# Attention scores as 64 by 64 quarters of the TensorE array instead of zero-padded full-array matmuls

## The chip, the core and the metric

The kernel runs on one NeuronCore of a Trainium2 chip. The metric is the time of one execution on the device in microseconds; lower is better. The engines named here are TensorE (PE for its matmuls, PEld for its weight loads), VectorE (DVE), ScalarE (ACT), GpSimd (POOL) and SyncE (SP), whose queue issues all the DMAs of this kernel.

## The reference

A local attention with block summaries is followed by two feed-forward blocks. Inputs are float32. There are 2 batches, 8 heads, 768 positions and a head size of 64.

```python
k_sum = k.reshape(B, H, nb, 32, D).max(axis=3)          # 24 blocks
v_sum = v.reshape(B, H, nb, 32, D).mean(axis=3)
scores_l = where(|i - j| < 16, q @ k.T / 8, -1e9)
scores_s = q @ k_sum.T / 8 + log(32)
a = softmax(concat([scores_l, scores_s]))
x = a @ concat([v, v_sum])                              # to (1536 tokens, 512)
x = x / sqrt(mean(x * x) + 1e-6) * rms_g
x = (silu(x @ w_gate) * (x @ w_val)) @ w_out            # d_ff 1536
h = x @ w_in
out = (s * relu(h) ** 2 + b) @ w_out2                   # d_ff 2048
```

## The kernel before, in words

**Attention.** The work is cut into 12 token tiles of 128 queries (index `i`; six to a batch) and 4 pairs of heads (`pr`), so 48 units. The two heads `e` of a pair lie on partitions 0 to 63 and 64 to 127 of queries and keys. A unit sees 192 key columns (`KC`): 24 block maxima, 8 columns of padding, 16 + 16 neighbours on both sides and the 128 keys of the tile itself. A unit passes these steps:

- `emit_a` (L317): two score matmuls in float32 (L328), one for each head. The stationary operand is a column block of `qz`, the queries of the tile. Each token tile's `qz` holds two zero-padded copies: in copy `e` only the 64 partitions of head `e` carry queries, and the others are zero, so that a matmul over all 128 partitions gives one head's scores. Both results go side by side into one PSUM bank. `top` (L333) then adds the mask on VectorE, writes the negated, scaled scores to the tile `P` in SBUF and leaves the maximum of each row in `sm`; `exps` (L339) takes the exponential on ScalarE with the row sums.
- `emit_b` (L345), three steps later: three transposes of `P` (L348), copied to `PT` by ScalarE or VectorE.
- `emit_c` (L361), six steps after the scores: three value matmuls (L367 to L369). After the fourth pair, `emit_d` normalises the token tile, and some ticks later `emit_e` (L396) transposes it for the feed-forward part.

**Order.** All is emitted in an order written by hand; every engine takes its instructions in that order. `attn` (L404) is a generator that yields twice a step: after `emit_b` and `emit_c`, and after `emit_a`. Each yield is a tick of the main loop (L640), which first runs what falls due (`run_due`). `after(d, fn)` puts `fn` in a list that is run d + 1 ticks on; `top` is put there with 1 and `exps` with 2. Between the ticks the main loop inserts groups of feed-forward matmuls (`gate` and `val`, twelve passes of 512 columns each), so that these begin while the attention goes on. Each group of them calls `run_due` too, through `slot` (L474).

**PSUM.** `banks(...)` hands out named banks in turn, and a bank taken again is waited for until all readers of its last contents are done. The scores take banks 0, 1 and 2 up to tick 20 (L631) and banks 0 and 1 after it (L644); the transposes use 3, 4 and 5 (later 3 and 4), the values 6 and 7, and the feed-forward groups 2 and 5.

**Queries.** There are two `qz` tiles, used in turn by the token tiles. `load_q` (L268) fills one with two DMAs of 64 partitions on the queue of SP; the load for tile `i + 2` is issued behind the scores of tile `i`. The zero halves are set once by four VectorE memsets at the start (L114, L115).

**Feed-forward.** From L615 on the rest of the two blocks runs, with float32 products as three float32r passes of hi and lo parts (L469 to L472, L601 to L604). It begins after the attention is done, and the change does not touch it.

Of the kernel before, what the change touches and what calls it, by code (L numbers as in the profile page):

```python
# [9 lines left out]
F32 = mybir.dt.float32  # L10
# [3 lines left out]
AF = mybir.ActivationFunctionType  # L14
ALU = mybir.AluOpType
AX = mybir.AxisListType
PSUM = bass.MemoryType.PSUM
# [3 lines left out]
NPAIR = NH // 2  # L21
NTL = SEQ // 128
# [3 lines left out]
KC = 192  # L26
# [10 lines left out]
def kernel(ctx: ExitStack, tc: tile.TileContext, q_t, k_t, v_t, v_w, w_gate, w_val, w_out, w_in2, w_out2, rms_g, s2, b2, out):  # L37
    nc = tc.nc
    scale = 1.0 / math.sqrt(HD)
# [16 lines left out]
    psp = pool("ps", 1, space=PSUM)  # L56

    def banks(*ids):
        """tiles of the PSUM banks ids, in turn"""
        turn = [0]  # L60

        def take():
            i = ids[turn[0] % len(ids)]
            turn[0] += 1
            return psp.tile([128, 512], F32, tag=f"b{i}", name=f"b{i}")
        return take
# [1 line left out]
    def r(ap):  # L68
        return ap.bitcast(F32R)

# [1 line left out]
    ident = const.tile([128, 128], F32, name="ident")  # L72
    mone = const.tile([128, NH], F32, name="mone")
    mhalf = const.tile([128, 1], F32, name="mhalf")
# [1 line left out]
    gbc = const.tile([128, DM], F32, name="gbc")  # L76
    sbc = const.tile([128, 1], F32, name="sbc")
    bbc = const.tile([128, 1], F32, name="bbc")
    qz = [const.tile([128, 2, NPAIR, 128], F32, name=f"qz{i}") for i in range(2)]
    part = const.tile([128, NSUB * 4 * SUB], F32, name="part")  # L80

    def big():
        return hgp.tile([128, NSUB * 2 * SUB], F32, tag="hg", name="hg")

    # keys and values of both batches lie where the products of the MoE come to lie later
    store = [big() for _ in range(5)] + [part[:, i * 3072:(i + 1) * 3072] for i in range(2)]
    kst = [t.rearrange("p (j c) -> p j c", c=KC) for t in (store[0], store[3], store[5])]
    vst = [t.rearrange("p (t a c) -> p t a c", t=3, a=NPAIR) for t in (store[1], store[2], store[4], store[6])]
# [2 lines left out]
    def kW(b, pr, t):  # L91
        j = (b * NPAIR + pr) * NTL + t
        return kst[j // 16][:, j % 16]

    def kpieces(b, pr):
        """runs of tiles of a pair's keys in one store: (store, slot, first tile, tiles)"""
        j = (b * NPAIR + pr) * NTL
        out, t = [], 0
        while t < NTL:
            n = min(NTL - t, 16 - (j + t) % 16)  # L100
            out.append((kst[(j + t) // 16], (j + t) % 16, t, n))
            t += n
        return out
# [6 lines left out]

    def consts():
        make_identity(nc, ident)
        for z in qz:
            nc.vector.memset(z[64:128, 0], 0.0)  # L114
            nc.vector.memset(z[0:64, 1], 0.0)  # L115
        for st in kst:
            nc.vector.memset(st[:, :, NS:BLK], 0.0)
        m = masks[1]
        nc.gpsimd.memset(m, 0.0)
        nc.gpsimd.memset(m[:, 0:NS], math.log(BLK) / scale)  # L120
        nc.gpsimd.memset(m[:, NS:BLK], NEG / scale)
        band(m, BLK, WIN, -WIN)
        band(m, BLK + WIN, WIN, 128)
        band(m, 64, 128, 0)
        for i, o in ((0, BLK), (2, BLK + WIN)):
            nc.vector.tensor_copy(masks[i], m)
            nc.vector.memset(masks[i][:, o:o + WIN], NEG / scale)
        nc.gpsimd.memset(mhalf, -0.5)
        nc.gpsimd.memset(mone, -1.0)
# [3 lines left out]
        nc.sync.dma_start(out=sbc, in_=s2.rearrange("(o d) -> o d", o=1).broadcast_to([128, 1]))  # L133
        nc.sync.dma_start(out=bbc, in_=b2.rearrange("(o d) -> o d", o=1).broadcast_to([128, 1]))

# [1 line left out]
    later = [[] for _ in range(8)]  # L137

    def after(d, fn):
        later[d].append(fn)  # L140
# [4 lines left out]
        for fn in due:  # L145
            fn()

# [1 line left out]
    order = []  # L149
    for m in range(KF):  # L150
        order.append(("s1", m))
# [26 lines left out]
        raw_t[i] = t  # L178

    def w_scale(i):  # L180
        """high words as float32 with their exponent moved: 2^-112 leaves five bits of it"""
        a = wap.tile([128, 512], F32, tag="wa", name="wa")
        nc.scalar.activation(out=a, in_=raw_t[i][:, :, 1].bitcast(F32), func=AF.Copy, scale=2.0 ** -112)
        a_t[i] = a

    def w_bits(i):
        """float32 of the float64 words: 23 bits of mantissa, the last one rounded to odd"""
        t = raw_t.pop(i)
        lo, hi = t[:, :, 0], t[:, :, 1]
        ai = a_t[i].bitcast(I32)  # L190
        ops = [
            lambda: nc.vector.tensor_scalar(out=ai, in0=ai, scalar1=3, scalar2=1, op0=ALU.logical_shift_left, op1=ALU.bitwise_or),
            lambda: nc.vector.scalar_tensor_tensor(out=ai, in0=hi, scalar=-0x80000000, in1=ai, op0=ALU.bitwise_and, op1=ALU.bitwise_or),  # L193
            lambda: nc.vector.scalar_tensor_tensor(out=ai, in0=lo, scalar=29, in1=ai, op0=ALU.logical_shift_right, op1=ALU.bitwise_or),  # L194
        ]
        pend[i] = ops

        def one():
            if ops:
                ops.pop(0)()  # L200
        one()
        if busy[0]:
            after(1, one)
            after(3, one)
        else:
            one()
            one()
# [27 lines left out]
                prog[j] += 1  # L235

    def w_ahead(part):
        """the weights' own work, between the work of the tokens"""
        i = used[0]
        if part == 0:  # L240
            w_to(i + 8, i + 7, 0, i + 5)
        elif part == 1:
            w_to(i + 8, 0, i + 6, 0)
# [6 lines left out]
        used[0] += 1  # L250
        return ready.pop(i)

# [1 line left out]
    vt_t = {}  # L254

    def load_k(b, pr):
# [9 lines left out]
        nc.sync.dma_start(out=vA[b][t].rearrange("p a c -> p (a c)"), in_=v_w[b, t])  # L266

    def load_q(i):  # L268
        z = qz[i % 2]
        for e in range(2):  # L270
            nc.sync.dma_start(out=z[64 * e:64 * e + 64, e].rearrange("p a c -> p (a c)"), in_=q_t[i, 64 * e:64 * e + 64])

    def prep_k(b, pr):
        ks = smallp.tile([128, NS], F32, tag="ks", name="ks")
# [10 lines left out]
        return vt_t[b][:, c0:c0 + 512].rearrange("p (a c) -> p a c", a=NPAIR)  # L285

    def prep_v(b, pr):
        """block means of the values, per column of the transposed values"""
        if pr == 0:
            nc.gpsimd.memset(vsums(b, 0), 0.0)  # L290
        vs = vsums(b, 1)[:, :, 0:NS]
        nc.vector.tensor_reduce(out=vs[:, pr], in_=vt_t[b][:, pr * SEQ:(pr + 1) * SEQ].rearrange("p (c i) -> p c i", i=BLK),
                                axis=AX.X, op=ALU.add)
        if pr == NPAIR - 1:
            for h in range(2):
                p0 = 64 * h
                nc.scalar.activation(out=vsums(b, 0)[p0:p0 + 64, :, p0:p0 + NS], in_=vs[p0:p0 + 64], func=AF.Copy, scale=1.0 / BLK)
# [16 lines left out]

    P_t, PT_t, X_t, xn_t, sm_t = {}, {}, {}, {}, {}

    def emit_a(i, pr, ps_s):  # L317
        t = i % NTL
        mk = masks[0 if t == 0 else 2 if t == NTL - 1 else 1]
        if pr == 0:  # L320
            sm_t[i] = smallp.tile([128, 2, NH], F32, tag="sm", name="sm")
        sm = sm_t[i]
        P = (tmpp.tile([128, 512], F32, tag="tmp", name="P") if i else wlp.tile([128, 512], F32, tag="wl", name="P"))
        P = P[:, 0:2 * KC].rearrange("p (e c) -> p e c", e=2)
        ps = ps_s()
        pv = [ps[:, e * KC:(e + 1) * KC] for e in range(2)]
        for e in range(2):
            nc.tensor.matmul(pv[e], qz[i % 2][:, e, pr], kW(i // NTL, pr, t), start=True, stop=True)  # L328

        def top():  # L330
            for e in range(2):
                h = 2 * pr + e
                nc.vector.tensor_tensor_reduce(out=P[:, e], in0=pv[e], in1=mk, op0=ALU.add, op1=ALU.min,  # L333
                                               scale=-scale, scalar=3.0e38, accum_out=sm[:, 0, h:h + 1])

        def exps():
            for e in range(2):
                h = 2 * pr + e
                nc.scalar.activation(out=P[:, e], in_=P[:, e], func=AF.Exp, scale=-1.0,  # L339
                                     bias=sm[:, 0, h:h + 1], accum_out=sm[:, 1, h:h + 1])  # L340
        after(1, top)
        after(2, exps)
        P_t[i, pr] = P

    def emit_b(i, pr, ps):  # L345
        P = P_t.pop((i, pr)).rearrange("p e c -> p (e c)")
# [55 lines left out]
        after(1, lambda: nc.vector.tensor_tensor(out=r(x[:, 1, :, c0:c0 + 128]), in0=pv, in1=x[:, 0, :, c0:c0 + 128], op=ALU.subtract))  # L402

    def attn(ps_s, ps_t, ps_x):  # L404
        """half a unit per step; yields the token tile that it completes"""
        loads = [lambda t=t: load_vw(0, t) for t in range(3, NTL)]
        loads += [lambda pr=pr: load_k(1, pr) for pr in range(NPAIR)]
        loads.append(lambda: load_vt(1))
# [31 lines left out]
        for s in range(n + LC):  # L440
# [14 lines left out]
                        emit_d(i)  # L455
            yield done
            if s < n:
                emit_a(*us[s], ps_s)
                i, pr = us[s]
                if pr == NPAIR - 1 and i + 2 < NT:  # L460
                    load_q(i + 2)
                yield

# [1 line left out]
    def mm12(ps, w, act):  # L465
        hi, lo = w
        for kk in range(4):
# [4 lines left out]
            nc.tensor.matmul(ps, r(hi[:, kk * 128:(kk + 1) * 128]), r(act(kk, 1)), start=False, stop=kk == 3)  # L472

    def slot(part):  # L474
        """what follows a group of products: the weights ahead, then older groups' work"""
        run_due()
        if phase:
            part = phase[0] = 1 - phase[0]
        if not busy[0]:
            w_ahead(part)  # L480
# [6 lines left out]
        return big().rearrange("p (s e c) -> p s e c", s=NSUB, e=2)  # L487

    def two(ps, dst, bias=None):
        """ps (+ bias) as a float32r pair"""  # L490
        if bias is None:
            nc.scalar.activation(out=r(dst[0]), in_=ps, func=AF.Copy)
            nc.vector.tensor_tensor(out=r(dst[1]), in0=ps, in1=dst[0], op=ALU.subtract)
# [2 lines left out]
            nc.vector.scalar_tensor_tensor(out=r(dst[1]), in0=ps, scalar=bias, in1=dst[0], op0=ALU.add, op1=ALU.subtract)  # L496

    def moe(x, ps_m):
        """x: a tile of (hi, lo) per part of the tokens"""
        hs, gs, y = {}, {}, []  # L500
        yp = part.rearrange("p (m s c) -> p m s c", m=KD, s=NSUB)
        op = part.rearrange("p (t c) -> p t c", t=NT)
# [112 lines left out]
        for kind, m in order:  # L615
            yield from {"s1": s1, "s2": s2, "s3": s3, "s4": s4}[kind](m)

# [1 line left out]
    consts()  # L619
    x = [xyp.tile([128, 2, KD, SUB], F32, tag="xy", name="x")]  # L620
    load_k(0, 0)
# [6 lines left out]
    for t in range(3):  # L628
        load_vw(0, t)
    load_small()  # L630
    m_banks, s_banks, t_banks = [banks(2, 5)], [banks(0, 1, 2)], [banks(3, 4, 5)]  # L631

    def ps_t():
        return t_banks[0]()
# [49 lines left out]
def _layout(q, k, v, moe_w_gate, moe_w_val, moe_w_out, moe_rms_g, moe2_w_in, moe2_w_out, moe2_s, moe2_b):  # L684
# [2 lines left out]
    c = np.ascontiguousarray  # L687

    def heads(a):
        # [b, h, s, d] -> [b, (e d), pair, s]  # L690
        return a.reshape(NB, NPAIR, 2, SEQ, HD).transpose(0, 2, 4, 1, 3).reshape(NB, 128, NPAIR, SEQ)

    qt = heads(q).reshape(NB, 128, NPAIR, NTL, 128).transpose(0, 3, 1, 2, 4)
# [63 lines left out]
```

## Time and profile before

| | |
|---|---|
| median of the runs shown (663.47 and 663.69) | 663.58 us |
| span of the profiled execution, first to last instruction | 662.4 us |
| the median over that span | 1.2 us more (the profiled execution's own time is not listed apart) |
| PE busy | 645.8 us, 97% of the span, 3140 passes |
| PEld busy | 547.7 us, 83% |
| DVE busy | 402.2 us, 61% |
| ACT busy | 272.6 us, 41% |
| POOL busy | 137.3 us, 21% |
| granted TensorE clock, mean | 0.997 of full |

Busy time counts the time in which an engine worked on at least one instruction. TensorE passes overlap (a pass is still on its way out while the next streams in), so a busy share near 100% says that the stream has no holes longer than such a tail, and the distance between two starts says what a pass costs. The profile lists one record for each pass; where the same kind of instruction follows itself, a timeline merges the records into one row with their count. A line number is that of the kernel above.

### The profile page before, as it was taken

To read this page: it belongs to the slowest core of one execution; us is meant where nothing else is said; L and a number is where in the kernel's file an instruction comes from. 1 tells how busy PE (TensorE), PEld (TensorE's weight loads), DVE (VectorE), ACT (ScalarE), POOL (GpSimd) and SP (SyncE) were. 2 spreads that over 40 slices of the span, in tenths; PEclk is the share of its full clock that TensorE was granted. 3 is DMA by queue.
4 is the path that set the end of the run, shared out by engine and by line. 5 is a ranking of instruction groups with operands and counts; after the bars stand their busy time and mean duration, and the time that the engine had idled before them with its cause. 6 is when DMAs were issued, how large, how long until landed. Compare 5 with 4: busy or idle time off the path is not lost.

```text
span 662.4 us, 8488 instructions
## 1 busy us (share of the span) xinstructions
PE 645.8 (97%) x3140; PEld 547.7 (83%) x3140; DVE 402.2 (61%) x763; ACT 272.6 (41%) x610; POOL 137.3 (21%) x157
## 2 busy tenths in 40 slices
PE   3989999999999999999999999999999999999998
PEld 3988999888888888888888888888888888888886
DVE  7699777469751355554455767882178637854632
ACT  3888767235433333321233335552455035403400
POOL 2365633213211111111111111110221022102100
PEclk9999999999999999999999999999999999999999
DMA  9995230014332121222222212113022202220022
GB/s 299 301 347 167 65 120 9 0 45 147 95 96 63 33 64 64 64 63 66 63 69 62 71 53 64 65 63 96 0 96 64 95 13 84 65 63 1 1 95 96
DMA packets 23243, 56.13 MB, mean 85 GB/s; under 512 B 2465, under 2 KB 8865, under 8 KB 23201
## 3 DMA queue, kind: packets, MB, share of 16 engines
q1 hardware_dynamic: 23200, 55.58, 26.4%
q8 instruction: 25, 0.41, 0.3%
q14 instruction: 18, 0.14, 0.1%
HBM read 52.43 MB, written 3.15 MB: 84 GB/s over the span
## 4 chain that ended last, share of the span: by engine, by line
PE 91%; ACT 2%; DMA 2%; DVE 2%; POOL 1%; issue 1%; SPq 0%; POOLq 0%
PE b L469 21%; PE b L470 21%; PE b L472 21%; PE b L601 7%; PE b L604 7%; PE b L602 7%; PE b L328 3%; DMA qz<-in_q_t_dram 2%; PE b L348 1%; ACT P L339 1%; PE b L367 1%; PE b L369 1%; PE b L368 1%; PE b L396 1%; ACT PT L354 0%
## 5 line engine op out<-in xcount | busy, mean ns | idle before, releaser
L216 POOL TENSOR_TENSOR wl<-wa,wh 128x512 fp32r<-128x512 f32 x68 | 90.5, 1338 | 418.4 <-ACT wh L214 328.8
L469 PE MATMUL b<-x,wh 128*128 128x512 f32 x288 | 113.1, 393 | 0.0
L470 PE MATMUL b<-x,wl 128*128 128x512 f32 x288 | 112.1, 389 | 0.0
L214 ACT ACTIVATE wh<-wa 128x512 fp32r<-128x512 f32 x68 | 41.5, 626 | 90.8 <-PE b L604 45.5
L472 PE MATMUL b<-x,wh 128*128 128x512 f32 x288 | 77.1, 389 | 0.0
L602 PE MATMUL b<-wl,hg 128*128 128x512 f32 (+1 forms) x196 | 75.1, 385 | 0.0
L601 PE MATMUL b<-wh,hg 128*128 128x512 f32 (+1 forms) x196 | 75.1, 385 | 0.0
L469 PE MATMUL b<-y,wh 128*128 128x512 f32 x192 | 74.7, 389 | 0.0
L470 PE MATMUL b<-y,wl 128*128 128x512 f32 x192 | 74.7, 389 | 0.0
L583 DVE SCALAR_TENSOR_TENSOR b<-u,sbc 128x512 f32<-128x512 f32 x48 | 50.7, 1056 | 35.6 <-ACT u L582 35.6
L472 PEld LDWEIGHTS b<-x,wh 128*128 128x128 f32 x288 | 54.1, 188 | 11.3
L470 PEld LDWEIGHTS b<-x,wl 128*128 128x128 f32 x288 | 54.1, 188 | 11.0
L469 PEld LDWEIGHTS b<-x,wh 128*128 128x128 f32 x288 | 54.1, 188 | 11.0
L469 PE MATMUL b<-hg,wh 128*128 128x512 f32 x144 | 56.0, 389 | 0.0
L470 PE MATMUL b<-hg,wl 128*128 128x512 f32 x144 | 56.0, 389 | 0.0
L496 DVE SCALAR_TENSOR_TENSOR hg<-b,bbc,hg 128x512 fp32r<-128x512 f32 x48 | 35.9, 749 | 28.2 <-ACT hg L495 28.2
L604 PE MATMUL b<-wh,hg 128*128 128x512 f32 (+1 forms) x196 | 51.5, 385 | 0.0
L472 PE MATMUL b<-y,wh 128*128 128x512 f32 x192 | 51.3, 389 | 0.0
L610 DVE TENSOR_TENSOR part<-b,part 128x512 f32<-128x512 f32 (+1 forms) x37 | 24.4, 673 | 43.4 <-PE b L604 43.4
L495 ACT ACTIVATE hg<-b,bbc 128x512 fp32r<-128x512 f32 x48 | 33.0, 688 | 43.0 <-DVE b L583 43.0
L194 DVE SCALAR_TENSOR_TENSOR wa<-raw,wa 128x512 int32<-128x512 int32 x68 | 49.2, 724 | 2.1
L193 DVE SCALAR_TENSOR_TENSOR wa<-raw,wa 128x512 int32<-128x512 int32 x68 | 49.1, 722 | 2.3
(93 smaller groups left out, 1075.0 us busy)
## 6 DMA issues: line engine op xcount, KB each, us to landing
raw<-in_w_out_dram SPq DMA_DIRECT2D x28, 512.0 KB, 3.5
raw<-in_w_in_dram SPq DMA_DIRECT2D x16, 512.0 KB, 3.5
raw<-in_w_gate_dram SPq DMA_DIRECT2D x12, 512.0 KB, 3.8
raw<-in_w_val_dram SPq DMA_DIRECT2D x12, 512.0 KB, 3.5
hg<-in_v_w_dram SPq DMA_DIRECT2D x9, 512.0 KB, 7.7
qz<-in_q_t_dram SPq DMA_DIRECT2D x24, 128.0 KB, 4.8
vt<-in_v_t_dram SPq DMA_DIRECT2D x8, 384.0 KB, 6.5
out_dram<-part SPq DMA_DIRECT2D x11, 256.0 KB, 2.0
```

What stands on the lines that cost most here:

```text
L193: lambda: nc.vector.scalar_tensor_tensor(out=ai, in0=hi, scalar=-0x80000000, in1=ai, op0=ALU.bitwise_and, op1=ALU.bitwise_or),
L194: lambda: nc.vector.scalar_tensor_tensor(out=ai, in0=lo, scalar=29, in1=ai, op0=ALU.logical_shift_right, op1=ALU.bitwise_or),
L214: nc.scalar.activation(out=r(h), in_=a, func=AF.Copy)
L216: nc.gpsimd.tensor_tensor(out=r(lo), in0=a, in1=h, op=ALU.subtract)
L469: nc.tensor.matmul(ps, r(hi[:, kk * 128:(kk + 1) * 128]), xh, start=kk == 0, stop=False)
L470: nc.tensor.matmul(ps, r(lo[:, kk * 128:(kk + 1) * 128]), xh, start=False, stop=False)
L472: nc.tensor.matmul(ps, r(hi[:, kk * 128:(kk + 1) * 128]), r(act(kk, 1)), start=False, stop=kk == 3)
L496: nc.vector.scalar_tensor_tensor(out=r(dst[1]), in0=ps, scalar=bias, in1=dst[0], op0=ALU.add, op1=ALU.subtract)
L583: after(0, lambda u=u, ps=ps: nc.vector.scalar_tensor_tensor(out=ps, in0=u, scalar=sbc[:, 0:1], in1=u, op0=ALU.mult, op1=ALU.mult))
L601: nc.tensor.matmul(acc, gh, r(ws[e][0][:, cs]), start=e == 0, stop=False)
L602: nc.tensor.matmul(acc, gh, r(ws[e][1][:, cs]), start=False, stop=False)
L604: nc.tensor.matmul(acc, r(ge[e][:, 1]), r(ws[e][0][:, cs]), start=False, stop=e == 3)
```

## The change

Queries are no longer padded: `qz` has one copy, filled by one DMA of 128 partitions, and its memsets go. `emit_a` is called for every second pair and makes the scores of two pairs at once. Each head's scores are made by two matmuls, one for each half of the 128 queries: the stationary operand is 64 partitions (the head) by 64 columns (the half), the result lands on 64 partitions of the PSUM bank. There is one bank for each head `e`, which holds both pairs `j` side by side. So a group of two pairs has eight matmuls where two units had four. `top` and `exps` of the second pair are issued one tick after those of the first. The scores use banks 0 and 1 from the start. (Comments and docstrings are taken out too, which the diff below leaves out.)

```diff
-    qz = [const.tile([128, 2, NPAIR, 128], F32, name=f"qz{i}") for i in range(2)]
+    qz = [const.tile([128, NPAIR, 128], F32, name=f"qz{i}") for i in range(2)]
...
-        for z in qz:
-            nc.vector.memset(z[64:128, 0], 0.0)
-            nc.vector.memset(z[0:64, 1], 0.0)
...
     def load_q(i):
-        z = qz[i % 2]
-        for e in range(2):
-            nc.sync.dma_start(out=z[64 * e:64 * e + 64, e].rearrange("p a c -> p (a c)"), in_=q_t[i, 64 * e:64 * e + 64])
+        nc.sync.dma_start(out=qz[i % 2].rearrange("p a c -> p (a c)"), in_=q_t[i])
...
-    def emit_a(i, pr, ps_s):
+    def emit_a(i, pr0, ps_s):
...
-        ps = ps_s()
-        pv = [ps[:, e * KC:(e + 1) * KC] for e in range(2)]
-        for e in range(2):
-            nc.tensor.matmul(pv[e], qz[i % 2][:, e, pr], kW(i // NTL, pr, t), start=True, stop=True)
...
+        pe = [ps_s() for _ in range(2)]
+        for j in range(2):
             for e in range(2):
...
+                rows = slice(64 * e, 64 * e + 64)
+                for c in range(2):
+                    cols = slice(64 * c, 64 * c + 64)
+                    nc.tensor.matmul(pe[e][cols, j * KC:(j + 1) * KC], qz[i % 2][rows, pr0 + j, cols],
+                                     kW(i // NTL, pr0 + j, t)[rows], start=True, stop=True)
+
+        def soft(j):
+            pr = pr0 + j
...
+            def top():
+                for e in range(2):
+                    h = 2 * pr + e
+                    nc.vector.tensor_tensor_reduce(out=P[:, e], in0=pe[e][:, j * KC:(j + 1) * KC], in1=mk, op0=ALU.add,
+                                                   op1=ALU.min, scale=-scale, scalar=3.0e38, accum_out=sm[:, 0, h:h + 1])
...
+            after(1 + j, top)
+            after(2 + j, exps)
+            P_t[i, pr] = P
+        soft(0)
+        soft(1)
...
-                emit_a(*us[s], ps_s)
                 i, pr = us[s]
+                if pr % 2 == 0:
+                    emit_a(i, pr, ps_s)
...
-    m_banks, s_banks, t_banks = [banks(2, 5)], [banks(0, 1, 2)], [banks(3, 4, 5)]
+    m_banks, s_banks, t_banks = [banks(2, 5)], [banks(0, 1)], [banks(3, 4, 5)]
```

## Rows read from the trace of the kernel before

**Rows 1.** Busy time by stretches, TensorE: stretch and length (us), busy (records), clock, DMA, GB/s.
```profile
0.00:15.80 15.80, 5.74 (x23) 1.00 0.92 292
15.80:40.00 24.20, 24.06 (x175) 0.93 0.94 308
40.00:60.00 20.00, 16.75 (x130) 1.00 0.92 317
60.00:120.00 60.00, 60.00 (x425) 1.00 0.18 54
120.00:662.40 542.40, 539.20 (x2395) 1.00 0.20 64
```
**Rows 2.** Waits of TensorE, whole span: waiter, releaser, us in total, times, longest.
```profile
PE b L328 <- DMA qz<-in_q_t_dram: 10.1, 2, 7.8
PE b L328 <- DVE sm L333: 3.2, 3, 2.1
```
**Rows 3.** Timeline of TensorE, one unit: start, us to last end, line, shapes, count.
```profile
74.15 0.39 PE L369 MATMUL b<-hg,PT 128*128 128x64 f32 x2
74.37 0.87 PE L328 MATMUL b<-part,qz 128*128 128x192 f32 x4
75.08 0.49 PE L348 MATMUL b<-ident,P 128*128 128x128 f32 x3
...
75.80 0.39 PE L369 MATMUL b<-hg,PT 128*128 128x64 f32 x2
76.02 0.38 PE L328 MATMUL b<-hg,qz 128*128 128x192 f32 x1
```
**Rows 4.** Timeline of TensorE, the passes under way at 28.0 us.
```profile
27.77 0.49 PE L328 MATMUL b<-hg,qz 128*128 128x192 f32 x2
```
**Rows 5.** Instructions of line 328: count, duration in ns (least/median/most), first and last start.
```profile
L328 PEld LDWEIGHTS b<-hg,qz x128: 186/190/338, 7.8 to 108.4; 128*128 128x128 f32 x128
L328 PE MATMUL b<-hg,qz x128: 326/326/657, 7.8 to 108.6; 128*128 128x192 f32 x128
```
**Rows 6.** Busy time by stretches, line 328 alone: PE, then PEld, with the number of records.
```profile
15.80:40.00 24.20, 12.53 (x52) 9.24 (x53) 0.93 0.94 308
40.00:60.00 20.00, 7.83 (x36) 5.56 (x36) 1.00 0.92 317
60.00:120.00 60.00, 18.86 (x88) 13.81 (x88) 1.00 0.18 54
```
**Rows 7.** Timeline of TensorE, 43 to 60 us: score rows with idle time before them.
```profile
47.19 0.92 PE L328 MATMUL b<-hg,qz 128*128 128x192 f32 x4 [2.07 <-DVE sm L333]
...
53.19 0.92 PE L328 MATMUL b<-hg,qz 128*128 128x192 f32 x4 [0.45 <-DVE sm L333]
...
55.75 0.92 PE L328 MATMUL b<-hg,qz 128*128 128x192 f32 x4 [0.70 <-DVE sm L333]
```
**Rows 8.** Timeline of TensorE, 104.7 to 108.1 us: score rows.
```profile
104.74 0.87 PE L328 MATMUL b<-part,qz 128*128 128x192 f32 x4
...
106.39 0.87 PE L328 MATMUL b<-part,qz 128*128 128x192 f32 x4
...
108.04 0.38 PE L328 MATMUL b<-hg,qz 128*128 128x192 f32 x1
```
**Rows 9.** Timeline of VectorE, same stretch: ends of two units' score reductions.
```profile
106.51 0.09 DVE L333 DVE_READ_ACCUMULATOR2_ANT sm<- 128x1 f32 x1
...
107.86 0.08 DVE L333 DVE_READ_ACCUMULATOR2_ANT sm<- 128x1 f32 x1
```
**Rows 10.** Timeline of SyncE, its DMA issues of queries.
```profile
2.14 1.28 SPq L271 DMA_DIRECT2D qz<-in_q_t_dram  x2
...
8.33 1.19 SPq L271 DMA_DIRECT2D qz<-in_q_t_dram  x2
```
**Rows 11.** Timeline of TensorE, the first scores of the second token tile.
```profile
15.78 1.61 PE L328 MATMUL b<-hg,qz 128*128 128x192 f32 x4 [2.22 <-DMA qz<-in_q_t_dram]
```
**Rows 12.** Busy time by stretches, TensorE, 16 to 18 us.
```profile
16.00:18.00 2.00, 2.00 (x8) 0.50 1.02 419
```

More of the change, by code (lines that the diff above doesn't have):

```diff
@@ L315 @@
     P_t, PT_t, X_t, xn_t, sm_t = {}, {}, {}, {}, {}
-    def emit_a(i, pr, ps_s):
+    def emit_a(i, pr0, ps_s):
         t = i % NTL
         mk = masks[0 if t == 0 else 2 if t == NTL - 1 else 1]
-        if pr == 0:
+        if pr0 == 0:
             sm_t[i] = smallp.tile([128, 2, NH], F32, tag="sm", name="sm")
         sm = sm_t[i]
-        P = (tmpp.tile([128, 512], F32, tag="tmp", name="P") if i else wlp.tile([128, 512], F32, tag="wl", name="P"))
-        P = P[:, 0:2 * KC].rearrange("p (e c) -> p e c", e=2)
-        ps = ps_s()
-        pv = [ps[:, e * KC:(e + 1) * KC] for e in range(2)]
-        for e in range(2):
-            nc.tensor.matmul(pv[e], qz[i % 2][:, e, pr], kW(i // NTL, pr, t), start=True, stop=True)
-        def top():
-            for e in range(2):
[L332 to L343, printed above, removed]
@@ new lines, in emit_a, with exps @@
+        pe = [ps_s() for _ in range(2)]
+        for j in range(2):
+            for e in range(2):
+                rows = slice(64 * e, 64 * e + 64)
[5 more added lines that the diff above has]
+            pr = pr0 + j
+            P = (tmpp.tile([128, 512], F32, tag="tmp", name="P") if i else wlp.tile([128, 512], F32, tag="wl", name="P"))
+            P = P[:, 0:2 * KC].rearrange("p (e c) -> p e c", e=2)
+            def top():
[3 more added lines that the diff above has]
+                                                   op1=ALU.min, scale=-scale, scalar=3.0e38, accum_out=sm[:, 0, h:h + 1])
+            def exps():
+                for e in range(2):
+                    h = 2 * pr + e
+                    nc.scalar.activation(out=P[:, e], in_=P[:, e], func=AF.Exp, scale=-1.0,
+                                         bias=sm[:, 0, h:h + 1], accum_out=sm[:, 1, h:h + 1])
+            after(1 + j, top)
+            after(2 + j, exps)
+            P_t[i, pr] = P
```

## Prediction

> **What bounds the kernel now.** I read the views in this order: busy time by stretches, TensorE's waits, the score line by stretches, then single steps.
>
> The stretches [rows 1] show one long TensorE stream. From 60 to 120 us TensorE is busy for all of it, and from 120 us to the end for 539 of 542. Before 15.8 it is mostly empty (5.7 us busy), from 15.8 to 40 it is full, from 40 to 60 it has holes of some 3 us. The waits [rows 2] name two causes only: the queries' DMA, 10.1 us, and the end of the score reduction on VectorE (L333), 3.2 us, which lies between 45 and 56 us [rows 7]. The clock is full except near 17 us [rows 12]. So whatever the change adds to or takes from TensorE behind 15.8 us goes into the total nearly one for one, except from 40 to 60, where VectorE holds it up. The 192 score records are 48 units (token tile by head pair) of four; 13 units lie between 15.8 and 40, 9 between 40 and 60, 22 behind 60 [rows 6]: 6.5, 4.5 and 11 groups of two.
>
> **What a unit costs.** A unit's two score matmuls appear as four passes, two to a matmul (every matmul between fp32 operands shows two passes in a row, L369 too [rows 3]). Two consecutive passes span 0.49 us and one lasts 0.326 [rows 4, 5], so they start 0.163 apart: that is the streaming of 192 columns. The other 0.163 of a pass is its tail behind the streaming. A unit takes 0.71 from its first pass to the next transpose [rows 3]: 4 x 0.163 = 0.65, and 0.06 in which the first weight load is not covered. For two L369 matmuls of 64 columns the distance is 0.22: one pair of weight load and matmul takes 0.11 however short its stream, so I take 0.11 for a load of 128 columns and, as an estimate, 0.056 for one of 64. Two units now cost 1.42.
>
> **The change, part by part.**
>
> *Quarters.* A group of two units issues 8 matmuls instead of 4, so 16 passes instead of 8, each still 192 columns long (0.163) and each on a quarter of the array. It gains only by running quarters side by side. The order of issue decides this: the code goes through (row half, column half) and each matmul brings both passes, high then low, to the *same* quarter. TensorE's records start in the order of issue [rows 3]. If that holds, the low pass waits until the high one has streamed, and the next quarter's high pass, behind it in order, starts together with it, not earlier. Each matmul then adds 0.163, not 0.326, and not 0.08: a group is 8 x 0.163 plus one last low pass, 1.47. That is what two zero-padded units cost now, and what the quarters save is spent on the two passes. Bounds of 16 passes from the nearest rows: 0.65 (four abreast) to 2.61 (one by one). I take 1.47: it follows from the order of starts that the rows show, and assumes of the quarters only that two can stream side by side.
>
> *Change of the array's shape.* Each group goes from the full array to quarters and back. No row shows this. Below it can be nothing. Above: the last matmul's tail of 0.163 must run out before the other shape's weights come, and that load is uncovered: 0.163 + 0.056 going in, 0.163 + 0.11 coming out, 0.49 a group. I take the upper end, because results of one shape still on their way out have to be told from those of the next, and every part of it has a row. The Trainium skill, "TensorEngine Tiling (Array Packing)", section "Key Properties", says that changing the tiling mode, not just the tile, drains the engine; no run here shows it yet. By that rule the upper end is right; without it the total would be some 9 us lower (17.5 groups by 0.49).
>
> So a group costs 1.47 + 0.49 = 1.96 in place of 1.42: **+0.54**. Behind 60 us: 11 x 0.54 = 5.9. From 15.8 to 40: 6.5 x 0.54 = 3.5, and the first group there runs at half clock [rows 11, 12], another 0.5. Before 15.8 two groups hide in the wait for the second tile's queries.
>
> *Banks.* Three (later two) banks in turn, one for each unit, become two banks that one group fills together. The next group's first matmul waits until the reductions of both units are done; the transposes, value products and MoE groups behind it on TensorE wait with it. Before, a unit waited for the unit two (or three) earlier. Behind 60 us this is covered: the units starting at 104.74 and 106.39 were reduced by 106.60 and 107.94, and the next pair began at 108.04 [rows 8, 9]. In the changed order the second reduction is issued one tick earlier, after TensorE's quarters end near 106.7, and takes 0.63, about 107.5, while the next group comes at 108.04 + 0.54. About 1 us is to spare. From 40 to 60, where VectorE is late already, the added 4.5 x 0.54 = 2.4 us of TensorE falls partly into the 3.2 us of waiting, but the tighter banks lengthen some waits. Bounds: nothing, and all 11 groups of 15.8 to 60 waiting 0.70, the middle one of the three waits [rows 7], 7.7. I take 1.2, half of the 2.4, because only three units of 22 wait there now.
>
> *Queries.* One DMA per token tile on 128 partitions instead of two on 64: SyncE saves about 0.6 us per tile (1.28 and 1.19 for two [rows 10]), one landing fewer in each ring of outstanding DMAs. Only the second tile's load is on the path: its issue began at 8.33 and TensorE waited until 15.78 [rows 10, 11]. If issue sets the landing, two saved issues bring 1.2; if bytes do (the DMA engines are 0.92 busy up to 15.8 [rows 1]), nothing. I take 0.3 off. The later loads are not waited for.
>
> *Memsets, names of helpers, earlier emission.* Four memsets leave VectorE before any key has landed; the wait for data covers them. VectorE's reductions and ScalarE's exponentials are as many and as long as before, and those of odd units come one tick earlier.
>
> **Sum.** 5.9 + 3.5 + 0.5 + 1.2 - 0.3 = 10.8 us. The profiled span is 662.4; the median of 663.58 is 1.2 above it, and I carry that over: **674 us**, 1.6% slower.
>
> **Rivals.**
>
> 1. *All four quarters run abreast, passes included.* For it: starts in order would need only a free queue in each quarter. Against it: nothing in the trace shows an overtaking. If loads are one behind another, 16 x 0.056 = 0.90, with the drain 1.39, no change: 663. Without the drain it is -0.52 over 17.5 groups, 654; with loads abreast too, 0.65, 650. The Trainium skill's same page, "Theoretical Speedup", promises up to 2x for each dimension of at most 64; that rule stands behind this rival, and no row bears it out. Chance 0.22.
> 2. *No overlap: slower.* The code gives slices, no array position, and it may be that quarters (or two that read the same rows) don't stream together; that is also the case in which the change doesn't do what it says. 16 x 0.163 = 2.61, with nothing to 0.49 of drain, +1.19 to +1.68 over 17.5 groups, 21 to 29, and 2 to 4 more from 40 to 60 after 3.2 us of its holes are filled: 687 to 697, about 692. It decides where the second quarter's high pass starts a whole pass after the first one's low pass. For it: no overlap of two matmuls' streams is seen in any row. Chance 0.17.
> 3. *The pair floor.* No load and matmul pair of the trace takes less than 0.11 [rows 3]. If that is issue and not loading, 16 pairs cost 1.76, with the drain 2.25, +0.83 over 17.5 groups, 14.5, and little else: 679. Chance 0.13.
> 4. *Gain and loss cancel*, or VectorE hides both: 664. Chance 0.05.
>
> My forecast (two abreast, drained) has 0.43; its own range, from no drain and no waits (664) to all waits (681), is 664 to 681.
>
> **Numbers.** A measurement of this kernel can tell about 2% from no change: below 650.3 is faster, above 676.9 slower. Faster: the best corner of rival 1, 0.05. Within: 0.29 of the forecast, 0.17 of rival 1, 0.03 of rival 3, 0.05 of rival 4, so 0.54. Slower: 0.14 of the forecast, 0.17 of rival 2, 0.10 of rival 3, so 0.41. The range of 656 to 688 leaves out the undrained end of rival 1 (0.07) and most of rival 2 (0.12).
>
> **What would show it.** In the changed profile the score line must have 384 passes of 64 by 64. Right: starts that come in couples, 0.163 between couples, 1.5 us from a group's first pass to its last end, and holes of 0.2 to 0.3 us before and after each group. Four starts within a few ns and then 0.163: rival 1. Starts evenly 0.163 apart: rival 2; evenly 0.11 apart: rival 3. The waits for L333 should stay below 6 us in all and lie before 60; if TensorE waits for L333 behind 60, I have mispriced the banks. The wait for the second tile's queries should end between 14.6 and 15.8. I am wrong if the stretch behind 120 us changes length at all, since nothing in it is touched.

## The result and the profile after

The changed kernel takes 670.05 us (669.35 and 670.75) against 663.58 before: a ratio of 1.0096, 95% interval 1.0067 to 1.0125. It is slower by 1%, within the 2% that count as no change here. The forecast was 674; its way and size are near, but two of its terms were wrong by more than 10 us each, in opposite directions.

The profiled execution has a span of 667.6 us. TensorE by stretches (columns as in [rows 1]), the kernel after:

```profile
0.00:15.80 15.80, 6.03 (x50) 1.00 0.91 320
15.80:40.00 24.20, 20.70 (x216) 1.00 0.96 340
40.00:60.00 20.00, 15.22 (x152) 0.90 0.64 257
60.00:120.00 60.00, 56.75 (x497) 0.98 0.16 54
120.00:667.60 547.60, 544.32 (x2436) 1.00 0.20 63
```

Before, the stream was full from 15.8 to 40 and from 60 to 120; now it has holes of 3.5 and 3.3 us there, and the clock is not full in two stretches between 49 and 63 (shown below). The length behind 120 us is longer by 5.2 (547.6 against 542.4) because attention work has slid into it: the stretch is not untouched, as I had assumed, it only starts later.

What a group of two units costs, kernel after, TensorE's timeline around one group (columns as in [rows 3]):

```profile
75.89 0.39 PE L374 MATMUL b<-hg,PT 128*128 128x64 f32 x2
76.20 0.88 PE L325 MATMUL b<-part,qz 64*64 64x192 f32 x16
77.01 0.55 PE L353 MATMUL b<-ident,P 128*128 128x128 f32 x3
```

The same kernel's timeline at the first instant of that group, weight loads (PEld) included:

```profile
76.00 0.28 PE L374 MATMUL b<-hg,PT 128*128 128x64 f32 x1
76.20 0.15 PEld L325 LDWEIGHTS b<-part,qz 64*64 64x64 f32 x4
76.20 0.39 PE L325 MATMUL b<-part,qz 64*64 64x192 f32 x4
```

Four passes together span 0.39 us, and one of them lasts 0.373: they start within 0.02 us of each other. The four rounds start at 76.20, 76.42, 76.58 and 76.74: 0.21 for the first, whose weight load is not covered, then 0.163 each, and with the last tail all 16 span 0.88. Loads are four abreast too (0.15 for four; one lasts 0.13). From the start of the last value pass (76.00) to the next transpose (77.01) it is 1.01, less the 0.11 that the value pass takes anyway: 0.90 us. The three transposes behind the group span 0.55 us where they spanned 0.49 [rows 3], since the first one's load is no longer covered. Together that is **0.96 us a group instead of 1.42**. Eleven groups behind 60 and eleven between 15.8 and 60 should have made the kernel 10 us faster.

They didn't, because TensorE now waits. Its waits, kernel after (columns as in [rows 2]):

```profile
PE b L325 <- issue: 10.2, 7, 2.8
PE b L325 <- DMA qz<-in_q_t_dram: 8.1, 2, 7.8
PE b L353 <- ACT P L342: 1.2, 1, 1.2
```

The line of 10.2 us is new. "issue" means that the profile names no releaser, but the times do. VectorE's timeline near 38 us, kernel after (a name in the brackets is what ended the idle time):

```profile
34.73 0.69 DVE L407 TENSOR_TENSOR x<-b,x 128x512 fp32r<-128x512 f32 x1
37.14 0.85 DVE L394 SCALAR_TENSOR_TENSOR xn<-xn,ss,gbc 128x512 f32<-128x512 f32 x1 [1.71 <-POOL ss L390]
37.91 0.35 DVE L336 CUSTOM_DVE_ANT_0 P<-b,mask 128x192 f32<-128x192 f32 x1
...
39.08 0.08 DVE L336 DVE_READ_ACCUMULATOR2_ANT sm<- 128x1 f32 x1
39.08 0.35 DVE L336 CUSTOM_DVE_ANT_0 P<-b,mask 128x192 f32<-128x192 f32 x1
39.36 0.08 DVE L336 DVE_READ_ACCUMULATOR2_ANT sm<- 128x1 f32 x1
```

TensorE's timeline over the same stretch:

```profile
37.39 0.39 PE L374 MATMUL b<-hg,PT 128*128 128x64 f32 x2
39.26 1.19 PE L325 MATMUL b<-hg,qz 64*64 64x192 f32 x16 [1.48 <-issue]
```

VectorE stands idle for 1.71 us at the scaling of a finished token tile (L394), whose root GpSimd has yet to deliver. The four reductions of the group whose scores are already made (L336) stand behind it. The last read of the first bank (head 0 of the second pair) ends at 39.16, and the next group's scores start at 39.26. The second bank is read to 39.44, and that group's 16 passes take 1.19 us instead of 0.88. The same 0.1 us lies between the last read of the first bank and the first pass at all seven waits. The first of them, 1.5 us at 10.85, lies ahead of the second tile's queries and costs nothing. The longest, 2.8 us at 48.73, is not idle time alone: behind a scaling that waited 1.32 us, VectorE prepares keys for 1.5 us before it comes to the reductions.

GpSimd is only the last link. Its row ahead of the scaling at 37.14, kernel after:

```profile
36.27 0.19 POOL L389 TENSOR_SCALAR ss<-ss 128x1 f32<-128x1 f32 x1 [1.79 <-ACT b L388]
```

GpSimd waited for ScalarE's sum of squares (L388), which ScalarE began at 35.47, behind four exponentials (two units).

VectorE's wait at the scaling, whole span, kernel before (columns as in [rows 2]):

```profile
DVE xn L389 <- POOL ss L385: 6.4, 9, 2.0
```

And in the kernel after:

```profile
DVE xn L394 <- POOL ss L390: 16.2, 12, 2.5
```

The long waits have a second cost. TensorE's clock by stretches, kernel after, around the waits that end at 48.73 and 58.85:

```profile
46.00:49.00 3.00, 0.27 (x4) 1.00 1.03 416
49.50:52.50 3.00, 3.00 (x20) 0.50 0.73 298
53.00:56.00 3.00, 3.00 (x38) 1.00 0.02 9
57.00:59.00 2.00, 0.15 (x2) 1.00 0.03 9
60.00:62.50 2.50, 2.50 (x15) 0.50 0.01 3
```

After each of the two near-empty stretches the granted clock is 0.50, the lower of its two levels (1.2 GHz), though TensorE is busy again; behind the first of them it is full from 53 to 56. Before the change this happened once, near 17 us [rows 12], in a part that waits for DMAs.

An account of my own from the trace sums the distances from start to start over the whole TensorE stream. Behind score passes they are 36.0 us before and 28.2 after. Ahead of a score group's first pass they are 11.3 and 15.0, although there are 22 such places instead of 45. Ahead of the transposes (not counting those directly behind scores) they are 19.0 and 27.3, of which 2.2 are 20 more steps of 0.11. All other lines add 1.1. In sum that is +5.3, which is the growth of the span. So the scores got shorter by 8 us, and the waits around them, at full or half clock, by more than that longer.

### The profile page after: what moved, and what is told of

Same layout as the page of the kernel before. It is cut to its first block, busy times and chain, and to the rows that moved or that the text cites. A ratio compares the mean times of both kernels' runs of the same rounds, so it can differ in the third digit from the quotient of the medians.

```text
span 667.6 us, 8863 instructions
## 1 busy us (share of the span) xinstructions
PE 643.0 (96%) x3332; PEld 533.7 (80%) x3332; DVE 402.2 (60%) x759; ACT 271.0 (41%) x610; POOL 137.8 (21%) x157
## 4 chain that ended last, share of the span: by engine, by line
PE 91%; ACT 3%; issue 2%; DVE 1%; DMA 1%; SPq 1%; POOL 0%; ACTq 0%; POOLq 0%
PE b L475 21%; PE b L478 21%; PE b L476 21%; PE b L610 7%; PE b L608 7%; PE b L607 7%; PE b L325 3%; PE b L353 2%; ACT P L342 2%; PE b L372 1%; PE b L374 1%; DMA qz<-in_q_t_dram 1%; PE b L373 1%; PE b L401 1%; DVE xn L394 1%
## 5 line engine op out<-in xcount | busy, mean ns | idle before, releaser
L478 PEld LDWEIGHTS b<-x,wh 128*128 128x128 f32 x288 | 54.0, 188 | 11.3
L502 DVE SCALAR_TENSOR_TENSOR hg<-b,bbc,hg 128x512 fp32r<-128x512 f32 x48 | 35.9, 749 | 28.2 <-ACT hg L501 28.2
L342 ACT ACTIVATE P<-P,sm 128x192 f32<-128x192 f32 x96 | 42.6, 447 | 22.7 <-DVE sm L336 21.4
L191 DVE SCALAR_TENSOR_TENSOR wa<-raw,wa 128x512 int32<-128x512 int32 x68 | 49.3, 725 | 2.1
```

## Experiments

All comparisons are with runs of the kernel before on the same chip (664.79 us for the first four, 663.65 for the next four, 664.12 for the last).

**Grouping and banks without quarters.** The changed order and the two banks, but zero-padded queries and full-array passes. (The padded `qz`, its memsets and its two loads come back too, which the diff below leaves out.)

```diff
-                for c in range(2):
-                    cols = slice(64 * c, 64 * c + 64)
-                    nc.tensor.matmul(pe[e][cols, j * KC:(j + 1) * KC], qz[i % 2][rows, pr0 + j, cols], ...)
+                nc.tensor.matmul(pe[e][:, j * KC:(j + 1) * KC], qz[i % 2][:, e, pr0 + j], kW(i // NTL, pr0 + j, t), start=True, stop=True)
```

> This kernel has the changed order (two pairs of scores at once, one bank for each head, two banks in all, the second pair's reduction a tick later) but keeps the zero-padded queries and the four passes over the full array for each unit. If the two banks are what costs (theory), TensorE now waits for L336-like reductions before groups although its own stream is as long as before: slower than before by 4 to 12 us, 668 to 676. If the grouping is harmless and the quarters themselves cost (change of shape, clock) (rival), it is within 2 us of before, 662 to 666.

Measured: 670.71 us, ratio 1.0091 (1.0076 to 1.0106). The time is the theory's: the grouping alone costs as much as the whole change. TensorE's waits in that kernel:

```profile
PE b L327 <- DMA qz<-in_q_t_dram: 8.6, 2, 8.4
PE b L327 <- DVE sm L337: 7.3, 6, 2.3
```

Here the profile does name VectorE's reduction. And VectorE's own wait at the scaling is there as well:

```profile
DVE xn L395 <- POOL ss L391: 16.5, 12, 2.3
```

So the grouped order has its own pace, and score groups that are 10 us shorter in all gain nothing on top of it. Whether the two banks or VectorE's order is at fault this run does not tell.

**Four score banks.** Scores in banks 0, 1, 4, 5, transposes and feed-forward groups sharing 2 and 3.

```diff
-    m_banks, s_banks, t_banks = [banks(2, 5)], [banks(0, 1)], [banks(3, 4, 5)]
+    shared = banks(2, 3)
+    m_banks, s_banks, t_banks = [shared], [banks(0, 1, 4, 5)], [shared]
...
-        if tick == 20:
-            s_banks[0], t_banks[0] = banks(0, 1), banks(3, 4)
```

> The changed kernel with four score banks taken in turn (0, 1, 4, 5), so that a group waits for the group two earlier; the transposes and the feed-forward groups share banks 2 and 3 in turn. If the waits before groups come from the two banks (theory), most of the 11 us of idle time before score groups goes, the half-clock stretches go with it, and the quarters' 0.51 us a group is kept: 651 to 657. If VectorE is the limit of the attention in any case (rival), the same waiting turns up at other instructions: 664 to 670.

Measured: 678.72 us, ratio 1.0200 (1.0169 to 1.0232; four runs from 676.55 to 680.88), slower than either expectation. TensorE's waits there:

```profile
PE b L325 <- DMA qz<-in_q_t_dram: 8.3, 2, 8.0
PE b L353 <- DVE hg L499: 4.1, 3, 2.1
PE b L353 <- ACT P L342: 3.0, 3, 1.5
PE b L353 <- DVE x L407: 2.9, 2, 2.1
```

The waits for the reductions are gone from the top, and others stand ahead of the transposes. The 4.1 us are for a bank that a feed-forward group still holds, the 2.9 for one that a token tile's transposes hold, and the 3.0 for the exponentials. VectorE still waits 15.4 us at the scaling. The run shows that taking banks from the others is no remedy; it does not tell what more banks alone would bring, since all eight are in use. So it leaves open what part the two banks have.

**The same quarter twice in a row.**

```diff
-        for j in range(2):
+        for _ in range(1):
             for e in range(2):
...
-                    nc.tensor.matmul(pe[e][cols, j * KC:(j + 1) * KC], qz[i % 2][rows, pr0 + j, cols],
+                    for j in range(2):
+                        nc.tensor.matmul(pe[e][cols, j * KC:(j + 1) * KC], qz[i % 2][rows, pr0 + j, cols],
...
```

> The changed kernel with the order of the eight matmuls turned: both pairs of one quarter come one after the other before the next quarter. If a quarter's passes wait in a queue of their own and other quarters overtake them (theory), four passes still start within some 20 ns of each other and a group lasts 0.65 us from first to last start as now; time as the changed kernel, 669 to 671. If matmuls start in the order of issue and one that waits for its quarter holds up those behind it (rival, the step of my prediction, moved from passes to matmuls), the four quarters start one after another 0.33 us apart, a group lasts about 1.5 us, and the time is 672 to 682.

Measured: 669.89 us, ratio 1.0083 (1.0053 to 1.0113). TensorE's timeline of a group in that kernel:

```profile
77.76 0.90 PE L326 MATMUL b<-part,qz 64*64 64x192 f32 x16
78.59 0.55 PE L354 MATMUL b<-ident,P 128*128 128x128 f32 x3
```

At its first instant:

```profile
77.76 0.41 PE L326 MATMUL b<-part,qz 64*64 64x192 f32 x4
```

With two matmuls, four passes, of one quarter issued ahead of the next quarter's first, the four quarters still start within 0.04 us and the group takes 0.90. (The expectation's 0.65 is four times 0.163, not the distance from first to last start, which is 0.56 us in the changed kernel and 0.58 here.) A matmul that waits for its quarter does not hold up those behind it that go to other quarters. The rival, my own step, is refuted.

**Both reductions in the first tick.**

```diff
-            after(1 + j, top)
-            after(2 + j, exps)
+            after(1, top)
+            after(2, exps)
```

> The changed kernel with the second pair's reduction and exponential issued in the same ticks as the first pair's, one tick earlier. If the wait for the banks is set by where the second reduction stands in VectorE's order (theory: there is a tick too little), the idle time before groups falls by 2 to 6 us: 664 to 668. If VectorE reaches both reductions late for other reasons (it is behind with other work, so that they already follow each other directly) (rival), nothing changes: 669 to 671.

Measured: 669.13 us, ratio 1.0068 (1.0053 to 1.0083). About 1 us at most; the theory of the missing tick fell. Near 38 us the four reductions follow each other almost directly already, behind the same wait, and VectorE's wait at the scaling is still 11.1 us.

**The scaling three ticks later.** That left VectorE's order. Before the change the reductions of one unit stood between the normalisation (L379) and the scaling (L389) in ten of the twelve token tiles. VectorE's timeline before, at its longest wait there:

```profile
26.17 0.69 DVE L379 TENSOR_TENSOR xn<-b,sm 128x512 f32<-128x512 f32 x1 [1.04 <-PE b L369]
26.81 0.36 DVE L333 CUSTOM_DVE_ANT_0 P<-b,mask 128x192 f32<-128x192 f32 x1
...
29.44 0.86 DVE L389 SCALAR_TENSOR_TENSOR xn<-xn,ss,gbc 128x512 f32<-128x512 f32 x1 [1.99 <-POOL ss L385]
30.22 0.34 DVE L333 CUSTOM_DVE_ANT_0 P<-b,mask 128x192 f32<-128x192 f32 x1
```

In the grouped order no reduction stands between the two in any tile, and in ten of the twelve all four of a group stand behind the scaling, as those near 38 us above. Four kernels, of which the first is the changed one with this edit:

```diff
-        after(3, lambda: nc.vector.scalar_tensor_tensor(out=xn, in0=xn, scalar=ss[:, 1:2], in1=gbc, ...))
+        after(6, lambda: nc.vector.scalar_tensor_tensor(out=xn, in0=xn, scalar=ss[:, 1:2], in1=gbc, ...))
```

> The changed kernel with one edit: VectorE's scaling of a finished token tile, which waits for GpSimd's root, is issued three ticks later, behind the reductions of the next group. Theory: VectorE stands 15.3 us at that instruction (6.4 before the change) with the reductions of the next group behind it, and TensorE then waits for the two banks; with the wait out of the way TensorE keeps most of the quarters' 11 us: 652 to 658, waits before score groups under 3 us. Rival (the two banks alone, whatever VectorE does): VectorE's wait goes, TensorE's stays, 666 to 670.

Measured: **658.61 us**, ratio 0.9916 (0.9898 to 0.9934). VectorE's wait at the scaling there:

```profile
DVE xn L394 <- POOL ss L390: 0.4, 2, 0.2
```

TensorE's waits there:

```profile
PE b L325 <- DMA qz<-in_q_t_dram: 8.1, 2, 7.8
PE b L325 <- issue: 2.4, 3, 1.5
PE b L353 <- ACT PT L359: 1.5, 4, 0.5
```

The 10.2 us are 2.4, of which 1.5 lie at 10.9, ahead of the second tile's queries, and TensorE's clock is full from 40 to 120 in that run. One edit on VectorE, with the banks as they are, takes 11 us off the changed kernel: the rival is out. The time is 0.6 us above the upper end expected.

The kernel before with the same edit:

> The kernel before with the same edit alone, as control. Theory: before the change VectorE's 6.4 us there stand hardly in TensorE's way (TensorE waited 3.2 us in all), so no more than that comes back: 660 to 664. Rival (the later scaling is a gain of its own, not tied to the grouping): 652 to 658, as far below as with the quarters.

Measured: 663.72 us, ratio 1.0000 (0.9989 to 1.0010). Alone, the edit leaves the time as it was. It is not without effect. Three of TensorE's waits there:

```profile
PE b L328 <- DMA qz<-in_q_t_dram: 10.5, 2, 8.4
PE b L396 <- DVE xn L389: 1.0, 1, 1.0
PE b L328 <- DVE sm L333: 0.7, 1, 0.7
```

The wait for reductions falls from 3.2 us [rows 2] to 0.7, while the last tile's scaling costs 1.0 and the first queries landed some 0.6 later in the profiled execution (8.4 against 7.8). So VectorE's 6.4 us stood in TensorE's way for 2.5 us at most; the kernel before with the last tile left in its place was not run.

The grouped kernel with full-array passes and the same edit:

> The grouped kernel on two banks with full-array passes (padded queries) and the scaling later. Theory: the grouping's loss of 6 us goes with VectorE's wait, and TensorE's stream is as long as before the change: 661 to 665, some 8 to 11 us above the quarters with the same edit. Rival (quarters bring nothing, the attention is not TensorE's to shorten): the same time as the quarters with this edit within 2 us.

Measured: 663.56 us, ratio 0.9996 (0.9985 to 1.0008). The grouping is harmless now, so its loss of 6 us was that wait. Between this kernel and the one with quarters, with order and banks alike, lie 5.0 us (663.56 less 658.61): what the quarters are worth here. It is less than the 8 to 11 expected. A group takes 1.36 us in the one and 0.96 in the other (medians over the groups behind 15.9 us, with the transposes' 0.06), 0.40 by 22 groups or 8.8 us. The two profiled spans differ by 6.0, and some 0.8 of that lies ahead of the first score pass, where the wait for queries is 8.5 and 7.8 us long. So the array is worth some 5 us of the 8.8. The rest went into waits, with the quarters, inside groups (0.87 us from first to last start instead of 0.56 where the second bank comes free later) and ahead of transposes; I did not take it apart further.

The changed kernel with both edits:

> The changed kernel with the scaling later and both reductions of a group in the first tick. Theory: once VectorE does not stand still, the tick that the second reduction gives away counts a little: 0 to 3 us below the run with the scaling later alone. Rival (the second tick is covered by what TensorE does between groups): the same within 1 us.

Measured: 659.88 us, ratio 0.9943 (0.9925 to 0.9961). No gain, rather 1.3 us the other way, just outside the rival's band and with intervals that overlap; the second tick is covered.

**All but the last tile.** In the run with the scaling later TensorE waits 1.0 us for the last tile's scaling, where no scores follow.

```diff
-        after(6, lambda: ...
+        after(3 if i == NT - 1 else 6, lambda: ...
```

> The quarters with the scaling three ticks later for all token tiles but the last, whose scaling keeps its place. In the run with all of them later TensorE waits 1.0 us for the last tile's scaling near 125 us; behind the last tile there are no more score groups to hold up. Theory: that 1.0 us comes back and nothing else changes, 657 to 658. Rival (the wait only moves to another instruction of the tail): 658.5 to 659.

Measured: **657.40 us**, ratio 0.9897 (0.9881 to 0.9914), 1% below the kernel before and about 2% below the changed one; the wait for the last tile's scaling is gone from TensorE's waits. It is the fastest version here, though its interval overlaps that of the run with all tiles later.

## Why the prediction was right in sum and wrong in its steps

- *Passes held up by the order of issue* (a group's stream of 1.47 us): wrong. The quarters took the passes four abreast, 0.56 and 0.58 us from the first to the last of 16 starts, in the two orders of issue. This was rival 1, to which I gave 0.22; four starts within 0.02 us rule out rivals 2 and 3 as well. The rows that I went by show starts in the order of issue where every matmul uses the whole array; they could not show what happens where the next one has a place of its own. The Trainium skill, "TensorEngine Tiling (Array Packing)", section "Key Properties", says that tiles operate independently, loads and matmuls alike; the trace agrees (four loads in 0.15 us, four passes within 0.02), and I should have given it more than 0.22 against an argument from rows of another kind.
- *Change of shape, 0.49 a group*: wrong in size. Going in, 0.20 from the last value pass's start to the first quarter's, where two such passes are 0.11 apart; coming out, 0.25 where a pass takes 0.163, and 0.06 for the first transpose's uncovered load. That is 0.24 a group. The Trainium skill, in that same section, says that changing the tiling mode drains the engine; the trace agrees nearly, since the first load of the new shape is recorded only 0.07 to 0.08 us before the end of the old shape's last pass (76.20 against 76.00 + 0.28, 77.01 against 76.20 + 0.88). The term was too large because 0.09 us a side, not a whole tail of 0.163, is lost, and because the load going in was not covered before either.
- *Group cost*: 0.96 measured, 1.96 predicted. The sum counted 17.5 groups, +9.4; over all 22 the trace says -10. (The two L369 matmuls of the prediction are the two passes of one matmul; the 0.11 for a pass and its load stands.)
- *Banks, 1.2 us, with 7.7 as upper end, all before 60*: wrong, and a miss of more than 10 us with what follows from it. The waits ahead of scores are 10.2 us in seven places, 8.7 of them behind 15.8, and they go on to 112 us. The step that failed is that I asked whether the reductions of units 42 and 43 would be done in time [rows 8, 9], at a place where VectorE does not stand at a scaling, and priced the waits by those of TensorE before [rows 7]. VectorE's waits I did not read: it had 6.4 us at the scaling, which reached TensorE for 2.5 us at most while one unit's reductions stood ahead of it. My own mark, TensorE waiting for the reductions behind 60, came out as the sign that the banks were mispriced. What the runs put in its place is more narrow: not the two banks alone but the reductions of a whole group behind one instruction that waits for GpSimd and, through it, ScalarE. (A slip on the way: 106.7 and 0.63 make 107.3, not 107.5; nothing hangs on it.)
- *Clock*: the two stretches at half clock were not in the sum. Twice some 3 us at half speed cost about 3 us. The 0.5 for a slow first group did come: the 16 passes of the row below take 1.67 us instead of 0.88, though the clock column prints 1.00 there.
- *Queries*: the second tile's scores start at 14.95 instead of 15.78 [rows 11], within the 14.6 to 15.8 I gave. The later stretches were indeed free of DMA waits. TensorE's timeline, kernel after:

```profile
14.95 1.67 PE L325 MATMUL b<-hg,qz 64*64 64x192 f32 x16 [0.34 <-DMA qz<-in_q_t_dram]
```

- *Nothing behind 120 changes*: the feed-forward passes did not (554.6 us from start to start before, 554.4 after), but the attention's end now lies in that stretch.

So 674 against 670 is luck: an error of about 19 us (the group, +9.4 forecast and -10 found) was nearly made up by one of about 15 the other way (1.4 us forecast for the first slow group, the banks and the queries together, some 16.5 found for all that is not the group). The range held since it took in rivals on both sides.

## What to carry to other kernels

When work is regrouped, read the waits of *every* engine in the chain, not of the bottleneck alone: a nearly harmless wait on an engine that works in order becomes the critical one once the work that frees the next group's buffers stands behind it and no free buffer is left. Before giving up a faster form of an instruction that brought no time, put the old form into the new order: here it was just as slow, which showed that the order was at fault, and moving one instruction turned +1% into -1%. A result near the forecast proves none of its terms; check each by its own row.

## What the hardware showed that I had not expected

- Quarters of 64 by 64 take float32 matmuls four abreast, with both passes of each. 16 passes take 0.88 us from first start to last end, less than the 1.30 (8 by 0.163) that eight full-array passes stream, and the order in which the quarters' matmuls are issued made no difference (0.88 and 0.90).
- Going from the full array to quarters and back costs some 0.24 us in all: 0.09 on each side and 0.06 for an uncovered load.
- Two near-empty stretches of 2 to 3 us were each followed by some 3 us at the lower clock level, while TensorE was busy again; in the run with the scaling later, which does not have these holes, the clock is 1.00 from 40 to 120 us.
